# The third stage's order: the gate's priority, the row load's priority and size, and the priority of the columns' low part

## The chip, the cores and the metric

The kernel runs on one core of a Trainium2 chip. Its time is the device time of one execution in microseconds (us). Before the change three runs gave 611.12, 612.05 and 613.5 us, a median of 612.05. The engines are named as in the profile: PE (TensorE's matmuls), PEld (its weight loads), DVE (VectorE), ACT (ScalarE), POOL (GpSimd) and SP (which here only issues transfers).

## The reference, cut to what matters

```python
attn = scan(x, a, B, C)                    # 4 batches x 8 heads x 768 steps x 32
x = attn.reshape(3072, 256)                # rows of 256

h = x @ w_in                               # 256 -> 2048
g = P3(h) / (Q2(h) + 1e-6)                 # a cubic over a quadratic, by element
x = g @ w_out                              # 2048 -> 256

logits = norm(x) @ norm(expert_emb).T / tau    # 3072 x 8
idx, w = argmax(logits), softmax(logits)[argmax]
for e in range(8):                         # w1[e] 256 x 1024, w2[e] 1024 x 256
    rows = idx == e
    out[rows] = w[rows] * (relu(x[rows] @ w1[e]) @ w2[e])
```

## The kernel before

Stage 1 (the scan) and stage 2 (the dense layers, 3072 rows in blocks) fill PE up to about 425 us; stage 2 also scatters each row, with its eight logits and its number, into a table in HBM ordered by expert. **Stage 3** takes the experts one after the other from that table and is what the change touches. A *slot* is an expert by its rank in row count, a tile is 128 rows, a *pass* is one slot's turn over some tiles.

The first three passes (`first_pass`, names `f...`: `fh` the hidden product, `fr` its ReLU, `fy` the output product, `fg` the rows) take two tiles each of slots 0, 1 and 2 with plain weights. The later passes (`run_pass`) are, in order, 0_2, 1_2, 2_2 (two tiles, starting at tile 2), 4_0, 5_0, 6_0, 7_0 (three tiles), 3_0 (twice two tiles). Names carry slot, first tile and chunk: `eh0_2_3` is slot 0, from tile 2, chunk 3 of the 1024 hidden units.

In a later pass each matrix is split into a high and a low part, and a product is made of three matmuls, high by high, high by low, low by high.

- **Weights** (L930 to L953): a load by SP into one of four buffers "raw" (`ra` for w1, `rb` for w2, L946), the high part by ACT (`eah`, `ebh`, L947), and the low part by a subtract of 128x512 on DVE or on POOL, whichever the planner finds free (`eal`, `ebl`, L950). The first passes' rows `fg` use the same four buffers until their last tile is delivered.
- **Rows** (L955 to L979): one load per pass by SP into one of three buffers `g` (L961); for each tile two transposes on PE into a PSUM bank (`t3`, L969; two such banks, which `ck` at L1180 uses too), the high part of the columns by ACT (`xh`, L972), the low part by DVE (`xl`, L975).
- **Gate** (L981 to L1009): from the rows, the norm and the logits, a chain of small steps between ACT (`jk`, L990, L995, L996, L1005) and DVE (L994, L997 to L1004, L1006 to L1008) that ends in the weight `gt` per row.
- **Hidden chunks** (L1011 to L1034): six matmuls into `eh` (L1023; PSUM, four banks), ReLU `hh` on ACT (L1025), the rest `hl` on DVE (L1026), then matmuls into `y` (L1032). Each pass has eight chunks.
- **Delivery** (L1036 to L1056): `y` times `gt` into `yo`, by ACT (L1046) or DVE (L1048), and an indirect transfer of the tile to `out`, issued by POOL (L1052).

**What sets the order.** Every instruction is recorded with `op(engine, duration, at, ...)`. `Plan.run` then replays them in a model of the five engines: an engine that is free takes the ready instruction with the smallest `at` whose buffers are free. `size` tells this model how long a transfer occupies it, and `port=True` (among these lines on L950 alone) that DVE and POOL exclude each other. The engines run the order that comes out; what the model thinks of times is gone by then, and only the waits on data and buffers remain. So a changed `at` can move any instruction that is ready at about the same model time. `sh(at, late, early)` adds `late` to `at` in stage 3.

Of the kernel before, what the change touches and what calls it, by code (L numbers as in the profile page):

```python
# [17 lines left out]
P = 128  # L18
# [10 lines left out]
ROW = DM + NE + 1  # L29
# [26 lines left out]
def sh(at, late, early):  # L56

    return at + (early if at < 4 else late)
# [16 lines left out]
class Plan:  # L75
# [29 lines left out]
    def op(self, eng, us, at, fn, r=(), w=(), lag=0.0, size=0, after=(), port=None):  # L105

        port = {None: ("POOL",), True: ("POOL", "DVE"), False: ()}[port]
        o = dict(port=port, on=eng if isinstance(eng, dict) else {eng: us}, any=isinstance(eng, dict), at=at, fn=fn, lag=lag, size=size, i=len(self.ops))
        deps = set()
        vals = {}
        for x, wr in [(x, False) for x in r] + [(x, True) for x in w]:
            v, s = x if isinstance(x, tuple) else (x, None)
            vals[id(v)] = v
            hit = lambda z: z[1] is None or s is None or z[1] == s
            deps.update(z[0] for z in v.wr if hit(z))
            if wr:  # L120
                deps.update(z[0] for z in v.rd if hit(z))
        for x, wr in [(x, False) for x in r] + [(x, True) for x in w]:
            v, s = x if isinstance(x, tuple) else (x, None)
            if wr:
                if s is None:
                    v.wr, v.rd = [], []
                else:
                    v.wr = [z for z in v.wr if z[1] != s]
                    v.rd = [z for z in v.rd if z[1] != s]
                v.wr.append((o["i"], s))  # L130
            else:
                v.rd.append((o["i"], s))
        deps.update(z[0] for v in after for z in v.wr + v.rd)
        deps.discard(o["i"])
        o["deps"] = deps
        o["vals"] = list(vals.values())
        for v in o["vals"]:
            v.left += 1
        self.ops.append(o)
        return o  # L140
# [135 lines left out]
def ssm_ffn_moe_kernel(  # L276
# [18 lines left out]
    D = nc.sync.dma_start  # L295
    plan = Plan()
    op = plan.op

    def act(n, k=0):
        return 0.06 + n / 1200 + 0.09 * k  # L300
# [5 lines left out]
    def dve(n, k=0):  # L306
        return 0.069 + n / 960 + 0.06 * k
# [20 lines left out]
    def bank(name, shape=(P, 512)):  # L328
        return plan.val(ps_s, list(shape), F32, name, "s", S_B, True)
# [95 lines left out]
    xs = dram.tile([NE * CAP, ROW], F32, name="xs")  # L425
    xs_v, xs_c = Val(tile=xs), Val(tile=xs)
# [97 lines left out]
    at = 26.0  # L524
# [340 lines left out]
    ranked = Val()  # L865
# [48 lines left out]
    one, two = Val(), Val()  # L914
# [40 lines left out]
    def tokens(e, t0, n, at):  # L955

        nm = f"{e}_{t0}"
        g = plan.val(sp, [P, TPE, ROW], F32, f"g{nm}", "g", 3)
        xh, xl = (plan.val(sp, [P, 2, TPE * P], FR, f"x{z}{nm}", f"x{z}", 2) for z in "hl")
        r0 = lambda: expert[e] * CAP + t0 * P  # L960
        op("SP", 0.47, sh(at - 4, 6.12, 0), lambda: D(out=g[:, 0:n, :], in_=xs[bass.ds(r0(), n * P), :].rearrange("(t p) c -> p t c", p=P)), r=[xs_v, xs_c, two, ranked], w=[g], size=n * P * ROW * 4)  # L961
        for t in range(n):
            tr = bank(f"t3_{nm}_{t}")
            o = slice(t * P, (t + 1) * P)
            tv = lambda tr=tr: tr[:, 0:256].rearrange("p (k t) -> p k t", k=2)

            def f(t=t, tr=tr):
                for k in range(2):
                    T.transpose(out=tr[:, k * P:(k + 1) * P], in_=g[:, t, k * P:(k + 1) * P], identity=ident.t)  # L969

            def f1(o=o, tv=tv):
                A.activation(out=xh[:, :, o], in_=tv(), func=AF.Copy)  # L972

            def f2(o=o, tv=tv):
                V.tensor_tensor(out=xl[:, :, o], in0=tv(), in1=xh[:, :, o].bitcast(F32), op=ALU.subtract)  # L975
            op("PE", 0.218, at - 2 + 0.3 * t, f, r=[g, ident], w=[tr])
            op("ACT", act(256), sh(at - 2 + 0.3 * t, 0.08, 0), f1, r=[tr], w=[(xh, t)])
            op("DVE", dve(256), sh(at - 2 + 0.3 * t, 6.92, 0), f2, r=[tr, (xh, t)], w=[(xl, t)])
        return g, xh, xl  # L979

    def gate(plan, nm, g, n, at, pool):  # L981
# [76 lines left out]
    def run_pass(e, t0, parts, at):  # L1058

        nm = f"{e}_{t0}"  # L1060
        g, xh, xl = tokens(e, t0, sum(parts), at)
        gt = gate(plan, nm, g, sum(parts), at + 1, sp)
        q = 0
        for n in parts:
            nm = f"{e}_{t0 + q}"
            y = [plan.val(*z, True) for z in [(ps_a, [P, 512], F32, f"y{nm}_{b}", "acc", 2) for b in range((n + 1) // 2)]]
            for f in range(8):
                hidden(nm, e, q, n, f, xh, xl, y, at + f * n / 4)
            at += 2 * n
            deliver(nm, q, n, g, y, gt, at + 0.9)  # L1070
            q += n
# [78 lines left out]
    at = S3  # L1150
    held = None
    for j, (e, t0, parts) in enumerate(FIRST + THEN):
        if j == len(FIRST):
            for g in range(NG - LATE, NG):
                route(g, NF * (g + 1) + 2)
            at += 4
        if j < len(FIRST):
            first_pass(e, EARLY, NF * (NG - 1) + 2 + 2 * j, 92.0 if j < SMALL else at, 1.2 if j < SMALL else 0.5, j < SMALL)
            at += 2 * EARLY if j >= SMALL else 0
            continue  # L1160
        if e != held:
            for i in range(8):
                weights(e, i, at - 7 + i, f"{e}_{t0}")
            held = e
        run_pass(e, t0, parts, at)
        at += 2 * sum(parts)
# [46 lines left out]
    with tc.If(n_over > 0), tc.tile_pool(name="ovp", bufs=1) as ovp:  # L1213
        def ot(shape, dt, name):
# [42 lines left out]
            out=ro, in0=lane[:, None, :].to_broadcast([P, NCH, P]), in1=sf[:, 1, :, None].to_broadcast([P, NCH, P]), op=ALU.is_equal,  # L1257
        )
        with tc.For_i(0, n_over, 1) as i:
# [14 lines left out]
            for k in range(2):  # L1274
                G.indirect_dma_start(
                    out=wa[:, k, :], out_offset=None, in_=w1.rearrange("e d f -> (e d) f"),
                    in_offset=bass.IndirectOffsetOnAxis(ap=wi[:, k:k + 1], axis=0),
                )
            for k in range(8):
                G.indirect_dma_start(  # L1280
                    out=wb[:, k, :], out_offset=None, in_=w2.rearrange("e f d -> (e f) d"),
# [20 lines left out]
            gt = gate(rest, "o", Val(tile=go), 1, 0.0, ovp)  # L1302
            rest.run()
            tr = ps_s.tile([P, 512], F32, name="tro", tag="s")
# [12 lines left out]
            for f in range(8):  # L1317
# [4 lines left out]
                out=out, out_offset=bass.IndirectOffsetOnAxis(ap=ti[:, 1:2], axis=0), in_=yv, in_offset=None,  # L1322
# [4 lines left out]
    with tc.If(n_odd > 0):  # L1327
        y_d = dram.tile([DM, NT], F32, name="y_d")
        with tc.tile_pool(name="gp", bufs=1) as gp:
# [30 lines left out]
        with tc.tile_pool(name="gq", bufs=1) as gq:  # L1360
# [21 lines left out]
            with tc.For_i(0, NT, 512) as t0:  # L1382
# [19 lines left out]
                for t in range(4):  # L1402
                    tr = ps_s.tile([P, 512], F32, name="trg", tag="s")
# [77 lines left out]
```

## Time and profile before

| | |
|---|---|
| median of three runs | 612.05 us (611.12 to 613.5) |
| the profiled execution | 609.87 us |
| its span, first to last instruction | 608.1 us |
| busy: PE, DVE, ACT, POOL | 550.6, 485.2, 467.4, 243.9 us |
| mean granted clock of PE | 0.973 of 2.4 GHz |
| from 430 to 444 us, PE busy | 14.00 of 14.00 us |
| from 556.0 to 595.6 us, PE busy | 39.60 of 39.60 us |
| from 595.6 us to the end of the span | 12.5 us, PE busy 0.02 |

The profiled execution's time is its span and 1.77 us around it. Shares of busy time are means over the whole span; the change lies in the last 180 us, so the views below are cut to windows there. In a timeline each row has a start, a duration, the engine, the line, the operation and its tiles; what stands in square brackets is how long the engine had been idle before it and what ended that.

### The profile page before, as it was taken

Reading aid. Unit: us, or ns where it says so; the run is one execution under the profiler, and the core shown is the slowest. Engines: PE = TensorE matmul, PEld = TensorE weight load, DVE = VectorE, ACT = ScalarE, POOL = GpSimd, SP = SyncE. Lnnn points to the kernel's source line nnn. Section 1 sums busy time; section 2 is a strip of 40 time slices with the busy share of each in tenths; the row PEclk is TensorE's granted clock in tenths of the full one; section 3 lists DMA queues with packets and bytes.
Section 4 is the critical chain, followed back from the end, with each engine's and each line's share of the span. In section 5 each row is a group of like instructions: output and inputs, shape, how many; then the busy total and the mean of one; then the engine's idle time right before and its main releaser. Section 6 shows DMA issues by size and latency. Waiting matters only on the chain.

```text
span 608.1 us, 10413 instructions
## 1 busy us (share of the span) xinstructions
PE 550.6 (91%) x3429; PEld 428.0 (70%) x3429; DVE 485.2 (80%) x994; ACT 467.4 (77%) x940; POOL 243.9 (40%) x229
## 2 busy tenths in 40 slices
PE   1567989999999999999999999899979979999991
PEld 0234656776667676767676786677869879999991
DVE  7998899889889998999899889883467676777430
ACT  6899989999999999989989997973255666566330
POOL 2573334445444544463454436342413442122111
PEclk9868999999999999999999999999999989999996
DMA  7960606122103110210010011961445645554000
GB/s 247 390 204 19 180 9 179 26 70 81 45 0 97 40 58 19 75 59 1 2 66 9 0 37 36 301 204 54 138 157 163 211 146 173 174 153 141 19 23 14
DMA packets 47919, 61.08 MB, mean 100 GB/s; under 512 B 4135, under 2 KB 37776, under 8 KB 47856
## 3 DMA queue, kind: packets, MB, share of 16 engines
q1 hardware_dynamic: 45360, 53.92, 28.9%
q0 software_dynamic: 2496, 6.41, 3.0%
q8 instruction: 29, 0.48, 0.3%
q14 instruction: 34, 0.28, 0.2%
HBM read 46.11 MB, written 14.72 MB: 100 GB/s over the span
## 4 chain that ended last, share of the span: by engine, by line
PE 53%; issue 14%; DVE 8%; DMA 7%; POOL 4%; ACT 3%; SPq 1%; POOLq 0%; DVEq 0%; ACTq 0%
PE acc L764 19%; PE h L738 19%; PE c L666 3%; DMA g<-xs 3%; PE y L706 2%; POOL out_dram L1052 2%; PE eh L1023 2%; PE fy L1118 1%; PE y L712 1%; PE tk L801 1%; PE y L1032 1%; DVE gh L752 1%; DMA out_dram<-yo,g 1%; DMA fg<-xs 1%; DVE u L753 1%
## 5 line engine op out<-in xcount | busy, mean ns | idle before, releaser
L755 POOL TENSOR_TENSOR gl<-p,v 128x512 fp32r<-128x512 f32 x96 | 126.8, 1324 | 173.7 <-DVE p L754 60.6
L738 PE MATMUL h<-x1h,wiw 128*128 128x512 f32 x384 | 142.0, 413 | 9.0 <-DVE p L754 5.9
L764 PE MATMUL acc<-gh,wow 128*128 128x512 f32 x384 | 112.0, 413 | 0.0
L738 PEld LDWEIGHTS h<-x1h,wiw 128*128 128x128 f32 x384 | 73.7, 192 | 35.3 <-DVE p L754 7.5
L764 PEld LDWEIGHTS acc<-gh,wow 128*128 128x128 f32 x384 | 67.9, 188 | 29.5 <-issue 15.9
L753 DVE SCALAR_TENSOR_TENSOR u<-u,lq,gh 128x512 f32<-128x512 f32 x96 | 81.1, 845 | 0.8
L752 DVE SCALAR_TENSOR_TENSOR gh<-h,as,v 128x512 fp32r<-128x512 f32 x96 | 71.6, 746 | 12.5 <-ACT v L750 12.0
L738 PE MATMUL h<-x1l,wiw 128*128 128x512 f32 x192 | 76.9, 401 | 0.0
L747 DVE SCALAR_TENSOR_TENSOR h<-p,sl,h 128x512 f32<-128x512 f32 x96 | 71.8, 749 | 6.0 <-ACT v L744 5.7
L743 ACT ACTIVATE p<-h,kk 128x512 f32<-128x512 f32 x96 | 65.3, 680 | 14.6 <-POOL gl L755 8.7
L754 DVE SCALAR_TENSOR_TENSOR p<-h,as,u 128x512 f32<-128x512 f32 x96 | 71.5, 745 | 3.0 <-DVE bw L651 0.2
L745 ACT ACTIVATE u<-v,qb 128x512 f32<-128x512 f32 x96 | 69.5, 724 | 1.5
L749 ACT ACTIVATE v<-u,lq 128x512 f32<-128x512 f32 x96 | 69.3, 722 | 1.6
L750 ACT ACTIVATE v<-v 128x512 f32<-128x512 f32 x96 | 60.4, 629 | 1.0
L764 PE MATMUL acc<-gl,wow 128*128 128x512 f32 x192 | 60.6, 396 | 0.1
L744 ACT ACTIVATE v<-h 128x512 f32<-128x512 f32 x96 | 56.9, 593 | 2.5 <-POOL gl L755 2.5
L1026 DVE SCALAR_TENSOR_TENSOR hl<-eh,hh 128x256 fp32r<-128x256 f32 (+1 forms) x72 | 34.3, 480 | 26.7 <-ACT hh L1025 26.2
L1032 PE MATMUL y<-ebh,hh 128*128 128x256 f32 x176 | 51.2, 291 | 1.3 <-ACT hh L1025 1.3
L1052 POOL DMA_INDIRECT out_dram<-yo,g x22 | 22.9, 1040 | 71.7 <-DVE yo L1048 51.6
L1032 PE MATMUL y<-ebh,hl 128*128 128x256 f32 x176 | 50.4, 286 | 1.1 <-DVE hl L1026 1.1
L1025 ACT ACTIVATE hh<-eh 128x256 fp32r<-128x256 f32 (+1 forms) x72 | 30.4, 424 | 26.0 <-PE eh L1023 23.5
L1032 PE MATMUL y<-ebl,hh 128*128 128x256 f32 x176 | 49.8, 283 | 0.0
(238 smaller groups left out, 1137.1 us busy)
## 6 DMA issues: line engine op xcount, KB each, us to landing
ra<-in_w SPq DMA_DIRECT2D x32, 256.0 KB, 3.0
rb<-in_w SPq DMA_DIRECT2D x32, 256.0 KB, 3.0
xb<-in_xb SPq DMA_DIRECT2D x12, 384.0 KB, 4.0
xs<-empty SPq DMA_DIRECT2D x8, 530.0 KB, 6.8
wiwr<-in_w_in SPq DMA_DIRECT2D x8, 512.0 KB, 7.3
wowr<-in_w_out SPq DMA_DIRECT2D x8, 512.0 KB, 7.5
xrow<-row SPq DMA_DIRECT2D x6, 530.0 KB, 3.6
bc<-in_bct SPq DMA_DIRECT2D x12, 256.0 KB, 2.8
```

The lines of the kernel that those rows point to most:

```text
L738: T.matmul(out=h.t, lhsT=part(wiw[g_], z)[:, k, fs], rhs=xx[:, k, :], start=(k == 0 and e == 0), stop=(k == 1 and e == 2))
L743: op("ACT", act(512, 1), s, lambda: A.activation(out=pp.t, in_=h.t, func=AF.Square, bias=kk.t), r=[h, kk], w=[pp])
L745: op("ACT", acts(512) + 0.06, s + 0.3, lambda: A.activation(out=uu.t, in_=vv.t, func=AF.Square, bias=qb.t), r=[vv, qb], w=[uu])
L747: op("DVE", dve(512, 1), s + 0.8, lambda: stt(out=h.t, in0=pp.t, scalar=sl.t, in1=h.t, op0=ALU.add, op1=ALU.mult), r=[h, pp, sl], w=[h])
L749: op("ACT", acts(512) + 0.09, s + 0.9, lambda: A.activation(out=vv.t, in_=uu.t, func=AF.Ln, bias=lq.t), r=[uu, lq], w=[vv])
L750: op("ACT", acts(512), s + 1.0, lambda: A.activation(out=vv.t, in_=vv.t, func=AF.Exp, scale=-1.0), r=[vv], w=[vv])
L752: op("DVE", dve(512, 1), s + 1.5, lambda: stt(out=gh.t, in0=h.t, scalar=as_.t, in1=vv.t, op0=ALU.add, op1=ALU.mult), r=[h, as_, vv], w=[gh])
L753: op("DVE", dve(512, 1), s + 1.6, lambda: stt(out=uu.t, in0=uu.t, scalar=lq.t, in1=gh.t.bitcast(F32), op0=ALU.add, op1=ALU.mult), r=[uu, l ...
L754: op("DVE", dve(512, 1), s + 1.7, lambda: stt(out=pp.t, in0=h.t, scalar=as_.t, in1=uu.t, op0=ALU.add, op1=ALU.subtract), r=[h, as_, uu], w ...
L755: op("POOL", pool2(512), s + 2.1, lambda: G.tensor_tensor(out=gl.t, in0=pp.t, in1=vv.t, op=ALU.mult), r=[pp, vv], w=[gl])
L764: T.matmul(out=acc[dh].t, lhsT=part(wow[g_], z)[:, i % 2, dh * P:(dh + 1) * P], rhs=x.t, skip_group_check=True, start=(i == 0 and e == 0), ...
L1032: T.matmul(out=y[t // 2][:, t % 2 * DM:(t % 2 + 1) * DM], lhsT=hx[:, o], rhs=wb[w][:, f % 2, :], start=(f == 0 and i == 0 and t % 2 == 0), ...
```

## The change

Three numbers of the order are changed; no computation is.

1. The rows' load (L961): its priority goes from `at - 4` with 6.12 added to `at - 6`, and the planner's model takes twice its real size.
2. The columns' low part (L975): 6.92 is no longer added to its priority, so that it follows 0.3 per tile from `at - 2`.
3. The gate (call at L1062): from `at + 1` to `at + 2 * parts[0] - 2`, which is `at + 2` in the passes of two tiles and 3_0, `at + 4` in those of three.

```diff
--- before.py
+++ after.py
@@ -958,7 +958,7 @@
         g = plan.val(sp, [P, TPE, ROW], F32, f"g{nm}", "g", 3)
         xh, xl = (plan.val(sp, [P, 2, TPE * P], FR, f"x{z}{nm}", f"x{z}", 2) for z in "hl")
         r0 = lambda: expert[e] * CAP + t0 * P
-        op("SP", 0.47, sh(at - 4, 6.12, 0), lambda: D(out=g[:, 0:n, :], in_=xs[bass.ds(r0(), n * P), :].rearrange("(t p) c -> p t c", p=P)), r=[xs_v, xs_c, two, ranked], w=[g], size=n * P * ROW * 4)
+        op("SP", 0.47, at - 6.0, lambda: D(out=g[:, 0:n, :], in_=xs[bass.ds(r0(), n * P), :].rearrange("(t p) c -> p t c", p=P)), r=[xs_v, xs_c, two, ranked], w=[g], size=2 * n * P * ROW * 4)
         for t in range(n):
             tr = bank(f"t3_{nm}_{t}")
             o = slice(t * P, (t + 1) * P)
@@ -975,7 +975,7 @@
                 V.tensor_tensor(out=xl[:, :, o], in0=tv(), in1=xh[:, :, o].bitcast(F32), op=ALU.subtract)
             op("PE", 0.218, at - 2 + 0.3 * t, f, r=[g, ident], w=[tr])
             op("ACT", act(256), sh(at - 2 + 0.3 * t, 0.08, 0), f1, r=[tr], w=[(xh, t)])
-            op("DVE", dve(256), sh(at - 2 + 0.3 * t, 6.92, 0), f2, r=[tr, (xh, t)], w=[(xl, t)])
+            op("DVE", dve(256), at + -2.0 + 0.3 * t, f2, r=[tr, (xh, t)], w=[(xl, t)])
         return g, xh, xl
 
     def gate(plan, nm, g, n, at, pool):
@@ -1059,7 +1059,8 @@
 
         nm = f"{e}_{t0}"
         g, xh, xl = tokens(e, t0, sum(parts), at)
-        gt = gate(plan, nm, g, sum(parts), at + 1, sp)
+
+        gt = gate(plan, nm, g, sum(parts), at + 2 * parts[0] - 2.0, sp)
         q = 0
         for n in parts:
             nm = f"{e}_{t0 + q}"
```

In the changed file a blank line shifts all lines behind L1061 by one (L1114 is L1115 there). The order on SP is the same but for one small load of a register that trades places with its neighbour. On PE two output products of pass 0_2 stand one chunk later. What moves is on DVE, ACT and POOL. Of the 64 subtracts of L950, 16 were on POOL and 20 are now.

On ScalarE, around the last first pass, the first delivery of slot 1 (`yo1_0_0`) stands ahead of two `jk` and two small steps of a gate that it stood behind, the ReLUs `fr2_0_3` and `fr2_0_6` have gone to VectorE, and the two `xh0_2` stand back to back behind `eah1_2_1`, where `ebh0_2_3` stood between them. Further on, `hh2_2_0` stands ahead of the first `jk4_0`, and stood behind it.

VectorE, around the last first pass (slot 2) and the start of pass 0_2; before:

```order
L1114 TENSOR_SCALAR fr2_0_5_5033<-fh2_0_5_5009 128x256
L950 TENSOR_TENSOR ebl1_2_0_5035<-rb1_2_0_4986,ebh1_2_0_5031 128x512
L950 TENSOR_TENSOR eal0_2_3_5043<-ra0_2_3_4993,eah0_2_3_5037 128x512
L950 TENSOR_TENSOR eal1_2_1_5056<-ra1_2_1_5023,eah1_2_1_5052 128x512
L1114 TENSOR_SCALAR fr2_0_7_5061<-fh2_0_7_5045 128x256
L975 TENSOR_TENSOR xl0_2_5069<-t3_0_2_0_5058,xh0_2_5067 128x2x128
L950 TENSOR_TENSOR ebl0_2_3_5078<-rb0_2_3_5041,ebh0_2_3_5071 128x512
L975 TENSOR_TENSOR xl0_2_5069<-t3_0_2_1_5073,xh0_2_5067 128x2x128
```

and after:

```order
L1115 TENSOR_SCALAR fr2_0_5_5029<-fh2_0_5_4996 128x256
L1007 TENSOR_SCALAR gt1_2_5023<-gt1_2_5023 128x2
L1008 RECIPROCAL gt1_2_5023<-gt1_2_5023 128x2
L1115 TENSOR_SCALAR fr2_0_6_5040<-fh2_0_6_5025 128x256
L1115 TENSOR_SCALAR fr2_0_7_5057<-fh2_0_7_5037 128x256
L975 TENSOR_TENSOR xl0_2_5063<-t3_0_2_0_5054,xh0_2_5061 128x2x128
L975 TENSOR_TENSOR xl0_2_5063<-t3_0_2_1_5069,xh0_2_5061 128x2x128
```

Four subtracts (`ebl1_2_0`, `eal0_2_3`, `eal1_2_1`, `ebl0_2_3`) no longer stand between the first pass's ReLUs and the columns `xl0_2`; one more ReLU (`fr2_0_6`) and two steps of a gate do.

GpSimd in the same place, where the deliveries of slots 0, 1 and 2 are issued (`fg` the rows whose buffer a delivery frees); before:

```order
L1052 DMA out_0_dram<-yo0_0_1_4851,fg0_0_4311 3072x256
L1052 DMA out_0_dram<-yo1_0_0_4952,fg1_0_4373 3072x256
L1052 DMA out_0_dram<-yo1_0_1_4968,fg1_0_4373 3072x256
L950 TENSOR_TENSOR ebl1_2_1_5104<-rb1_2_1_5050,ebh1_2_1_5081 128x512
L1052 DMA out_0_dram<-yo2_0_0_5106,fg2_0_4431 3072x256
L1052 DMA out_0_dram<-yo2_0_1_5116,fg2_0_4431 3072x256
```

and after:

```order
L1052 DMA out_0_dram<-yo0_0_1_4851,fg0_0_4311 3072x256
L1052 DMA out_0_dram<-yo1_0_0_4941,fg1_0_4373 3072x256
L1052 DMA out_0_dram<-yo1_0_1_4949,fg1_0_4373 3072x256
L950 TENSOR_TENSOR ebl0_2_2_4992<-rb0_2_2_4917,ebh0_2_2_4985 128x512
L950 TENSOR_TENSOR ebl1_2_0_5042<-rb1_2_0_5000,ebh1_2_0_5035 128x512
L950 TENSOR_TENSOR eal0_2_3_5050<-ra0_2_3_5009,eah0_2_3_5044 128x512
L950 TENSOR_TENSOR eal1_2_1_5065<-ra1_2_1_5018,eah1_2_1_5048 128x512
L1052 DMA out_0_dram<-yo2_0_0_5100,fg2_0_4431 3072x256
L1052 DMA out_0_dram<-yo2_0_1_5115,fg2_0_4431 3072x256
```

Three of the subtracts that left VectorE stand here now, with `ebl0_2_2`, as a block of four between two deliveries; `ebl1_2_1` left POOL.

VectorE at the start of pass 4_0, where that pass's gate meets the last chunks of pass 2_2; before:

```order
L1026 SCALAR_TENSOR_TENSOR hl2_2_3_5624<-eh2_2_3_5590,hh2_2_3_5611 128x256
L1000 TENSOR_SCALAR sq4_0_5553<-sq4_0_5553 128x3
L1001 RECIPROCAL rc4_0_5569<-sq4_0_5553 128x3
L1004 TENSOR_TENSOR ex4_0_5529<-ex4_0_5529,rc4_0_5569 128x24
L1026 SCALAR_TENSOR_TENSOR hl2_2_4_5648<-eh2_2_4_5617,hh2_2_4_5638 128x256
L975 TENSOR_TENSOR xl4_0_5654<-t3_4_0_0_5634,xh4_0_5646 128x2x128
```

and after:

```order
L1026 SCALAR_TENSOR_TENSOR hl2_2_3_5620<-eh2_2_3_5582,hh2_2_3_5609 128x256
L997 RECIPROCAL rc4_0_5626<-sq4_0_5596 128x3
L998 TENSOR_TENSOR rc4_0_5626<-rc4_0_5626,s24_0_5534 128x3
L999 TENSOR_TENSOR sq4_0_5596<-sq4_0_5596,rc4_0_5626 128x3
L1000 TENSOR_SCALAR sq4_0_5596<-sq4_0_5596 128x3
L1001 RECIPROCAL rc4_0_5626<-sq4_0_5596 128x3
L1026 SCALAR_TENSOR_TENSOR hl2_2_4_5647<-eh2_2_4_5613,hh2_2_4_5635 128x256
L975 TENSOR_TENSOR xl4_0_5652<-t3_4_0_0_5631,xh4_0_5644 128x2x128
```

Before, the gate's steps L997 to L999 stood further ahead, each between chunks of 2_2 and two subtracts, and `ex4_0` (L1004) ahead of `hl2_2_4`; now L997 to L1001 are one block behind `hl2_2_3`, and `ex4_0` comes behind the first `xl4_0`.

## Rows read from the trace of the kernel before

**Rows 1.** Waits of TensorE, 430 to 608: line waited for, total us, times, longest.

```profile
PE t L969 <- DVE xl L975: 3.5, 1, 3.5
PE ck L1180 <- DVE xl L975: 2.0, 1, 2.0
PE y L1032 <- ACT hh L1025: 1.3, 1, 1.3
PE y L1032 <- DVE hl L1026: 1.1, 2, 0.6
```

**Rows 2.** Windows: stretch, us, busy (instructions) of each engine, granted clock, DMA share, GB/s.

```profile
452.00:455.40 3.40, 1.35 (x10) 0.99 (x9) 1.90 (x5) 2.04 (x5) 0.00 (x0) 1.00 0.63 187
455.40:458.90 3.50, 3.50 (x17) 3.29 (x16) 3.36 (x13) 0.67 (x2) 2.08 (x2) 0.51 0.46 139
483.00:489.60 6.60, 5.29 (x43) 4.93 (x43) 4.60 (x15) 5.51 (x18) 2.24 (x2) 1.00 0.37 113
489.60:493.00 3.40, 0.34 (x3) 0.14 (x2) 3.33 (x5) 0.26 (x2) 2.63 (x3) 1.00 0.47 140
493.00:496.40 3.40, 2.97 (x14) 2.97 (x15) 2.38 (x9) 2.05 (x5) 0.25 (x1) 0.50 0.82 255
```

**Rows 3.** Timeline of TensorE: last first pass and start of pass 0_2.

```profile
454.84 0.24 PE L1180 MATMUL ck<-oh,ones 128*128 128x8 bf16 x4 [2.05 <-DVE xl L975]
...
455.96 0.78 PE L1023 MATMUL eh<-xh,eah 128*128 128x256 f32 x1
...
456.75 0.41 PE L1023 MATMUL eh<-xh,eal 128*128 128x256 f32 x1
456.96 0.41 PE L1023 MATMUL eh<-xh,eah 128*128 128x256 f32 x1
...
459.11 0.28 PE L1023 MATMUL eh<-xh,eal 128*128 128x256 f32 x1
459.23 0.28 PE L1023 MATMUL eh<-xh,eah 128*128 128x256 f32 x1
```

**Rows 4.** Timeline of ScalarE there.

```profile
444.70 0.45 ACT L1046 ACTIVATE yo<-fy,gt 128x256 f32<-128x256 f32 x1
...
452.77 0.63 ACT L947 ACTIVATE eah<-ra 128x512 fp32r<-128x512 f32 x1 [1.16 <-DMA ra<-in_w]
...
454.80 0.37 ACT L972 ACTIVATE xh<-t 128x256 fp32r<-128x256 f32 x1
```

**Rows 5.** Timeline of GpSimd there.

```profile
446.71 0.97 POOL L1052 DMA_INDIRECT out_dram<-yo,fg  x1 [0.31 <-DVE eal L950]
```

**Rows 6.** Timeline of SP there: loads' issue.

```profile
447.46 3.08 SPq L946 DMA_DIRECT2D ra<-in_w  x2
```

**Rows 7.** Chain that ended last, there: start, us, what.

```profile
450.17 2.58 DMA ra<-in_w
```

**Rows 8.** Timeline of VectorE there.

```profile
453.43 0.69 DVE L950 TENSOR_TENSOR eal<-ra,eah 128x512 fp32r<-128x512 f32 x1 [1.37 <-ACT eah L947]
...
454.93 0.69 DVE L950 TENSOR_TENSOR ebl<-rb,ebh 128x512 fp32r<-128x512 f32 x1
455.54 0.42 DVE L975 TENSOR_TENSOR xl<-t,xh 128x256 fp32r<-128x256 f32 x1
```

**Rows 9.** Line L950 on GpSimd, 435 to 608: count: min/median/max ns.

```profile
L950 POOL TENSOR_TENSOR eal<-ra,eah x7: 1276/1288/1310, 466.5 to 552.7; 128x512 fp32r<-128x512 f32 x7
```

**Rows 10.** Timeline of VectorE at the start of pass 4_0.

```profile
489.15 3.13 DVE L1000 TENSOR_SCALAR sq<-sq 128x3 f32<-128x3 f32 x1
...
492.96 0.42 DVE L975 TENSOR_TENSOR xl<-t,xh 128x256 fp32r<-128x256 f32 x1
```

**Rows 11.** Timeline of GpSimd at the start of pass 4_0.

```profile
489.76 1.28 POOL L950 TENSOR_TENSOR eal<-ra,eah 128x512 fp32r<-128x512 f32 x1
490.98 1.27 POOL L950 TENSOR_TENSOR ebl<-rb,ebh 128x512 fp32r<-128x512 f32 x1
```

**Rows 12.** Groups by form, 430 to 608: count, busy us, mean ns, idle before.

```profile
L998 DVE TENSOR_TENSOR rc<-rc,s 128x4 f32<-128x4 f32 x1 | 1.2, 1199 | 0.0
```

## The prediction

> **What bounds the kernel now.** The change lies in stage 3, so I read the waits of TensorE from 430 us on, then the windows around the longest, then the timelines of the engines in them. TensorE is busy without a gap through most of this stage; its waits are few, and four lines hold nearly all of them: 3.5 us before a transpose of pass 4_0, 2.0 before `ck`, 1.3 before an output product, and twice together 1.1 before another [rows 1]. All but the 1.3 end with VectorE. What the change is worth must come out of these 7.9 us and out of what follows them: behind the 2.0 the granted clock is 0.51 for 3.5 us, behind the 3.5 it is 0.50 for 3.4 us, and around the 1.3 it stays 1.00 [rows 2]; 0.5 is the lower of the two levels, 1.2 GHz of 2.4. At that level matmuls of a chunk start 0.21 us apart (456.75, 456.96), at the higher 0.12 (459.11, 459.23) [rows 3].
>
> **The rows' load (1).** The order on SP is the same but for one register load, so the earlier priority moves no transfer: the loads go out when their buffer comes free. The doubled size lives only in the planner's model. I cost the edit itself at nothing; what it does, it does by the other engines' order.
>
> **Columns and deliveries around 445 to 460 (2 and 3).** This is the largest term. Before, the chain runs: ScalarE makes `yo1_0_0` at 444.70 [rows 4], the second of slot 1's deliveries is issued by GpSimd at 446.71 [rows 5], and its end frees the buffer for the second of two loads on SP [rows 6], `ra1_2_1`, whose transfer takes from 450.17 to 452.75 [rows 7], 3.46 us behind the delivery's issue. ScalarE then has `eah1_2_1` at 452.77, and `xh0_2`, which is queued behind it, has its second half only at 454.80 [rows 4]. On VectorE the second `xl0_2` follows at 455.54, behind `ebl0_2_3` of 0.69 us, and ends at 455.96 [rows 8], where the first chunk of pass 0_2 starts [rows 3].
>
> After, `yo1_0_0` stands ahead of two `jk` and two small steps of a gate that it stood behind: I put it 1.5 us earlier, at 443.2, and the delivery's issue 1.7 earlier, at 445.0, because the subtract that stood in front of it is ordered away too. With the same 3.46 us the buffer would be free at 448.5. SP issues in order, and the load ahead of it (447.46 [rows 6]) waits for a buffer that `ebl0_2_2` frees, now a subtract on GpSimd of 1.29 us where VectorE took 0.69 [rows 8, 9]; that puts it at 448.2 and `ra1_2_1` at 448.8. It lands 2.58 later, at 451.4 (451.9 if the four subtracts on GpSimd hold anything up): 0.9 to 1.4 before now. Behind it `eah1_2_1` (0.63), two `xh0_2` (0.37 each), two `xl0_2` (0.42 each) with no subtract between: the last ends at 453.2 to 453.7. `ck` and the four matmuls of `fy` stand before the first chunk, which took from 454.84 to 455.96, 1.1 us [rows 3]; the first bank is free one `xl0_2` sooner, so the chunk starts at about 454.45. **Term: -1.5** (between -1.0 and -1.9).
>
> TensorE's one idle stretch of 2.05 us is then two of about 1.1 and 0.8. The trace has one idle stretch of 1.3 without a fall of the clock [rows 1, 2] and two of 2.05 and 3.49 us with one, so I take the clock to hold. The 17 matmuls of the window 455.4 to 458.9 [rows 2] then start 0.12 instead of 0.21 us apart [rows 3]: 17 x 0.094 = 1.6. **Term: -1.6** (0 if the clock falls all the same).
>
> Given back: pass 0_2's first output product needs `hl0_2_0`, and VectorE now has `ebl0_2_3` and `ebl1_2_1` ahead of it, which it had before or not at all; one of them, 0.69 [rows 8], is not covered by anything on TensorE. **Term: +0.7** (0 to 1.4).
>
> **The gate of pass 4_0 (3).** Before, one small step of the gate, `sq4_0` of 128x3 (L1000), holds VectorE from 489.15 for 3.13 us, to 492.28 [rows 10]. Beside it GpSimd runs two subtracts end to end, 489.76 to 492.25 [rows 11]; the step ends when they have. Behind it wait two more steps, `hl2_2_4` and the first `xl4_0`, which starts 0.68 later at 492.96 [rows 10]; the transposes need its bank and start after 3.49 us [rows 1]. After, the block L997 to L1001 stands at about the same time behind `hl2_2_3`, and the first of its steps with two operands in memory meets `eal4_0_3` on GpSimd, which is still followed by `ebl4_0_2`. I let GpSimd start them 0.7 sooner, about half of the 1.3 us that go ahead of it (below): VectorE is free at 491.6, the three steps left and `hl2_2_4` take 0.9 where two steps and `hl2_2_4` took 0.68, and `xl4_0` of 0.42 ends at 492.9; the transposes start some 0.4 sooner than now. **Term: -0.4.** The bounds are wide: if the block passes before GpSimd's first subtract, VectorE runs on and the whole wait goes with the slow clock behind it, -3.5 and, for the 14 matmuls in the slow stretch [rows 2], 14 x 0.094 = -1.3, in all -4.8; if all four steps are held, each behind a subtract of its own, two more subtracts come on top, +2.6. I take the middle that is nearest the row, because the same engines meet in the same order.
>
> The Trainium skill (SBUF — State Buffer, Who interferes with whom) has a rule for this: of VectorE and GpSimd the one that issues first has the shared ports for its whole instruction, and the other is blocked until then. By that rule the step would have waited for one instruction. The trace agrees on the block but not on its length: the step stayed blocked past a second start on GpSimd at 490.98 [rows 10, 11]. With one subtract alone VectorE would come free 1.3 us sooner, this term would be -1.7, and the sum 607.5 us in place of 608.8.
>
> The 1.3 us before an output product [rows 1] is `hh2_2_0` queued on ScalarE behind a gate's `jk4_0` that waits for its rows; in the new order it stands ahead. That wait goes, but TensorE then only comes sooner to the same blocked `xl4_0`, which is late next. **Term: 0.**
>
> **Later passes.** The smaller of the two waits for `hl` [rows 1] is about 0.4 (1.1 less 0.6 and rounding), at the turn from 4_0 to 5_0; the low part there now stands ahead of two subtracts. **Term: -0.4.** The larger, 0.6, comes from the gate step that took 1.2 us behind a single subtract on GpSimd [rows 12]. That subtract (`eal3_0_1`) is VectorE's now, but one at the turn before it (`eal7_0_1`) is GpSimd's: the same price a pass earlier. **Term: 0.** The four subtracts on GpSimd between pass 4_0 and 5_0 cost 5.2 us there [rows 9], beside work of TensorE that is full; nothing, unless a step of VectorE needs its ports (rival 2).
>
> **Sum.** -1.5 - 1.6 + 0.7 - 0.4 - 0.4 = -3.2 us against the profiled execution's 609.87: 606.7. The median of the runs shown is 2.2 above that execution, so on its scale 612.05 - 3.2 = **608.8 us**.
>
> **Rivals.**
> 1. *The clock falls at pass 0_2 all the same, or the loads bind.* For it: two idle stretches stand close together there, and the load before `ra1_2_1` comes later by GpSimd's slower subtract. Against it: the 1.3 us at 484. Then the 1.6 is not won: 610.4 us, no measurable change.
> 2. *VectorE is starved behind GpSimd's rows of subtracts: slower.* The order has two rows of four where before there were at most two side by side. For it: two end to end already held one small step for 3.13 us [rows 10, 11]. Four take 5.2 us; a gate step or a low part that arrives at their start while TensorE's next product hangs on it adds at least what two did: 3.5 of waiting and 1.3 of slow clock, 4.8. From one such stall on it decides, since the gains are 3.2: 612.05 - 3.2 + 4.8 = 613.7 us, with two 618.5. Against it: around 448 VectorE's work is mostly ReLUs out of PSUM, whose wait TensorE has 0.6 us or less of so far.
> 3. *Pass 4_0's stall dissolves.* For it: the gate's steps move to another place, and only a few tenths decide who comes first. Against it: they stay within the same 4 us. Then 4.8 less 0.4 more is won: 604.4 us.
> 4. *It doesn't do what it says.* The load that is to go sooner doesn't; if only noise in the order is left, the time is 612 within 1 us.
>
> **How the numbers follow.** The forecast has 0.40, rival 1 0.22, rival 2 0.16, rival 3 0.14, rival 4 0.08. Half a per cent, 3.06 us, is about what a measurement can tell from no change here. The forecast lies 3.25 below the median and so at that edge: 0.25 of its 0.40 count as faster, with 0.14 of rival 3 and 0.05 of rival 1 that is 0.44. Slower is rival 2 less the part that the gains make up for, 0.15 of 0.16 with the width of the measurement against it and a little from rival 4: 0.17. The rest, 0.39, is no change. The forecast's own range is 607 to 610.4, from the bounds of its terms. For 8 in 10 it is drawn down to rival 3 and up to one stall of rival 2: 603.9 to 613.8.
>
> **What would show it.** In the profile after: `ck` at 453 to 453.5 and the first chunk of 0_2 at 454 to 455; granted clock 1.00 from 455 to 459; the wait before the transposes of 4_0 still 3 us or more, behind a gate step of over 2 us on VectorE; no wait of TensorE over 1.5 us elsewhere; the wait of 1.3 at 484 gone. I am wrong if a wait of several us stands anywhere that has none now, or if the clock between 455 and 459 is still 0.5.

## The result and the profile after

The changed kernel took 606.98 us (median of 15 runs, 601.0 to 610.85) beside 611.12 (15 runs, 608.21 to 617.55) for the kernel before: ratio 0.9901, 95% interval 0.9877 to 0.9926 (the two medians alone give 0.993). In two later sessions the same pair gave 0.9911 (0.9885 to 0.9936) and 0.9941 (0.9911 to 0.9970). So the change takes off 0.6 to 1.0%, some 3.6 to 6 us (2.8 to 5.4 by the medians alone). Forecast were 3.2: the right sign, but less than the intervals of the first two sessions allow (4.5 to 7.5 and 3.9 to 7.0 us).

The profiled execution of the changed kernel lasts 609.72 us (span 607.9), no less than before's 609.87. That is no contradiction. The order is the same on every engine up to about 440 us, so up to there the executions differ by chance alone. One chunk of the first passes on TensorE, in the kernel before and then in the changed one (timeline: start, duration):

```profile
420.94 1.11 PE L1108 MATMUL fh<-fx,fa 128*128 128x256 f32 x4
```

```profile
426.15 1.57 PE L1109 MATMUL fh<-fx,fa 128*128 128x256 f32 x4
```

The changed kernel's profile came there 5.2 us late and ended 0.2 early: 5.4 us were won behind this point (5.9 from the second matmul of this chunk to the last one of the kernel). Over the first twelve profiles of the table below, the second matmul of this chunk starts anywhere between 419.5 and 426.7 us. A comparison of two profiled executions must therefore start at a common row near the change.

TensorE's waits in the changed kernel, 420 us to the end, answer to [rows 1]:

```profile
PE t L969 <- DVE xl L975: 3.6, 1, 3.6
PE ck L1181 <- DVE xl L975: 1.4, 1, 1.4
PE tk L799 <- ACT row L804: 1.2, 1, 1.2
PE y L1032 <- ACT hh L1025: 0.3, 1, 0.3
PE y L1032 <- DVE hl L1026: 0.2, 1, 0.2
```

The 3.5 us before the transposes of 4_0 are still there; the 1.3 for `hh` is gone (the 0.3 stands elsewhere), the 1.1 for `hl` has shrunk to 0.2; `ck` waits 1.4 in place of 2.0. (`tk` belongs to the part before the change.) The windows around `ck` and around 4_0, as in [rows 2]:

```profile
455.40:458.90 3.50, 2.14 (x15) 1.68 (x15) 1.50 (x6) 2.12 (x5) 2.79 (x3) 1.00 0.43 115
458.90:462.40 3.50, 3.50 (x32) 3.50 (x31) 2.90 (x9) 2.59 (x7) 2.17 (x2) 1.00 0.74 206
490.00:494.40 4.40, 0.85 (x8) 0.65 (x6) 4.26 (x10) 1.32 (x4) 3.06 (x3) 1.00 0.46 129
494.40:497.80 3.40, 3.39 (x20) 3.39 (x21) 1.99 (x8) 2.21 (x6) 2.50 (x2) 0.64 0.89 272
```

Behind `ck` the granted clock now stays at 1.00, and 32 matmuls run in 3.5 us where 17 ran; behind 4_0 it falls as before. Around `ck`, the changed kernel's timeline of ScalarE:

```profile
456.30 0.63 ACT L947 ACTIVATE eah<-ra 128x512 fp32r<-128x512 f32 x1 [0.46 <-DMA ra<-in_w]
456.84 0.64 ACT L972 ACTIVATE xh<-t 128x256 fp32r<-128x256 f32 x2
```

of VectorE:

```profile
457.24 0.76 DVE L975 TENSOR_TENSOR xl<-t,xh 128x256 fp32r<-128x256 f32 x2 [2.22 <-ACT xh L972]
```

and of GpSimd:

```profile
448.99 0.97 POOL L1052 DMA_INDIRECT out_dram<-yo,fg  x1 [0.30 <-DVE gt L1006]
```

From `eah1_2_1` to the end of the second `xl0_2` it is 1.7 us (456.30 to 458.00), where it was 3.2 (452.77 to 455.96 [rows 4, 8]): the two columns now follow each other. For the rest, count from the second matmul of the chunk above, at 421.24 and 426.72. The delivery is issued 22.3 us behind it (448.99), where it was 25.5 (446.71 [rows 5]), and `eah1_2_1` starts 29.6 us behind it (456.30), where it was 31.5 (452.77 [rows 4]). So delivery and weight both come sooner, the weight by less, since from the one to the other it is now 7.3 us and was 6.1.

At 4_0 the picture is that of [rows 10, 11] with another gate step in it, `L998` of 128x3. VectorE:

```profile
490.18 2.93 DVE L998 TENSOR_TENSOR rc<-rc,s 128x3 f32<-128x3 f32 x1
```

and GpSimd beside it:

```profile
490.59 1.28 POOL L950 TENSOR_TENSOR eal<-ra,eah 128x512 fp32r<-128x512 f32 x1
491.80 1.27 POOL L950 TENSOR_TENSOR ebl<-rb,ebh 128x512 fp32r<-128x512 f32 x1
```

### The profile page after: what moved, and what is told of

Same layout as the page of the kernel before. It is cut to its first block, busy times and chain, and to the rows that moved or that the text cites. A ratio compares the mean times of both kernels' runs of the same rounds, so it can differ in the third digit from the quotient of the medians.

```text
span 607.9 us, 10415 instructions
## 1 busy us (share of the span) xinstructions
PE 555.0 (91%) x3429; PEld 430.0 (71%) x3429; DVE 478.7 (79%) x989; ACT 467.1 (77%) x941; POOL 249.7 (41%) x233
## 4 chain that ended last, share of the span: by engine, by line
PE 59%; issue 8%; DMA 7%; DVE 7%; ACT 4%; POOL 3%; SPq 1%; another core or an unknown queue 0%; POOLq 0%; ACTq 0%
PE h L738 19%; PE acc L764 19%; PE eh L1023 4%; PE y L1032 4%; PE c L666 3%; DMA g<-xs 2%; PE y L706 2%; PE y L712 2%; DMA ra<-in_w 2%; POOL out_dram L1052 1%; PE tk L801 1%; PE fy L1119 1%; DMA out_dram<-yo,g 1%; DMA fa<-in_w 1%; DVE gh L752 1%
## 5 line engine op out<-in xcount | busy, mean ns | idle before, releaser
L764 PEld LDWEIGHTS acc<-gh,wow 128*128 128x128 f32 x384 | 68.0, 188 | 29.6 <-issue 15.9
L753 DVE SCALAR_TENSOR_TENSOR u<-u,lq,gh 128x512 f32<-128x512 f32 x96 | 78.9, 822 | 0.8
```

What stands on the lines that cost most here:

```text
L753: op("DVE", dve(512, 1), s + 1.6, lambda: stt(out=uu.t, in0=uu.t, scalar=lq.t, in1=gh.t.bitcast(F32), op0=ALU.add, op1=ALU.mult), r=[uu, l ...
L764: T.matmul(out=acc[dh].t, lhsT=part(wow[g_], z)[:, i % 2, dh * P:(dh + 1) * P], rhs=x.t, skip_group_check=True, start=(i == 0 and e == 0), ...
```

## Which of the edits moves the order

This needs no run: each edit alone, set beside the kernel before, row by row on every engine. The load's earlier priority alone gives the order of before. The columns' new priority alone gives the order of before. The doubled size alone gives the changed kernel's order but for eight rows on ACT, DVE and POOL, all where pass 4_0 begins; doubled size and columns' priority together give the changed kernel's order exactly, so the gate's new priority adds nothing to them. (Alone, the gate's priority moves rows from pass 4_0 on, and others than the change does.) What is timed first below is therefore a number in the planner's model of a transfer, nothing that the chip is told.

## The experiments

**The doubled size alone.**

```diff
-        op("SP", 0.47, sh(at - 4, 6.12, 0), ..., w=[g], size=n * P * ROW * 4)
+        op("SP", 0.47, sh(at - 4, 6.12, 0), ..., w=[g], size=2 * n * P * ROW * 4)
```

> Of the change only the doubled size of the rows' load in the planner's model; priorities of load, columns and gate as before. On ACT, DVE and POOL its order differs from the changed kernel's in eight rows, all at pass 4_0. Theory A (the doubled size alone makes the gain): ratio to before 0.990 +- 0.003, and in the trace the wait before ck 1.4 us, granted clock 1.00 behind it, the 3.5 us before the transposes of 4_0 still there. Rival B (the gate's or the columns' new priority is needed): at most a third of the gain, 0.997 or above.

Ratio 0.9963 (0.9936 to 0.9990): a gain, but less than theory A's, and less than the changed kernel's in its own session. So it was run again beside the changed kernel.

> The kernel of size_only once more, now beside the changed kernel in one session. It came out at 0.996, the changed kernel at 0.990 and 0.991, though their orders differ in eight rows at pass 4_0. Theory A (those rows, which the columns' new priority moves, are worth 2 to 3 us): 0.994 to 0.997 and 0.003 or more above the changed kernel beside it. Rival B (the rows are worth nothing, the executions scatter): within 0.002 of it.

> The changed kernel, unaltered, as the partner of the other three. Ratio 0.989 to 0.993; in the profile the waits that all its profiles had (3.5 us before the transposes of 4_0, about 1 before ck, none for hl above 0.3 in the later passes), and clock 1.00 at the start of 0_2.

0.9947 (0.9919 to 0.9975) beside 0.9941 (0.9911 to 0.9970), the changed kernel a little above what was expected of it; medians 604.70 and 605.51. Rival B of the repeat holds: the eight rows are worth nothing that was measured here, though intervals of 0.003 either way would hide 1.8 us. But for these rows the doubled size alone is the change. Its waits in the repeat, at the same two places:

```profile
PE t L969 <- DVE xl L975: 3.7, 1, 3.7
PE ck L1180 <- DVE xl L975: 0.9, 1, 0.9
```

**Early passes alone, later passes alone.** The size is doubled only for 0_2, 1_2 and 2_2 (first kernel), only for the passes from 4_0 on (second).

```diff
-        ..., size=n * P * ROW * 4)
+        ..., size=(2 if t0 == 2 else 1) * n * P * ROW * 4)    # size_first
+        ..., size=(1 if t0 == 2 else 2) * n * P * ROW * 4)    # size_later
```

> The doubled size only for the loads of passes 0_2, 1_2 and 2_2; all else as before. Theory A (two thirds or more of the gain comes from the order around 444 to 497 us, where the first pass's ReLUs and the columns xl0_2 no longer stand behind subtracts): ratio 0.992 to 0.994, no wait of TensorE for fr, wait before ck 1.4, clock 1.00 at the start of 0_2; the 0.4 and 0.6 us waits for hl at the later turns stay. Rival B (the gain is spread over the later passes): 0.997 or above.

> The doubled size only for the loads of passes 4_0, 5_0, 6_0, 7_0 and 3_0; all else as before, so the order around 444 to 460 is before's. Theory A: ratio 0.996 to 0.998 (the waits of 0.4 and 0.6 us for hl go, some 1.3 to 1.6 us), the 2.05 us before ck and the clock of 0.5 behind it stay. Rival B: 0.993 or below.

0.9976 (0.9953 to 0.9999) and 0.9977 (0.9959 to 0.9996), in the session in which both together (size_only) gave 0.9963. Each half is worth some 1.4 us, with intervals from about nothing to 2.9. Theory A's two thirds for the first half is not borne out, and its profile has a wait of 1.0 us for `fr` that was to be gone. The second half's ratio came as theory A expected, but not its reason in full: a wait of 0.6 for `hl` is left, and `ck` waited 1.54 with the clock at 1.00, not 2.05 with 0.5 behind it.

**The changed kernel again, and its block of four subtracts put back on VectorE.**

```diff
-            {"DVE": dve(512), "POOL": pool2(512)}, 0, sh(at, 7.77, 0),
+            {"DVE": dve(512)} if f"e{k}l{nm}_{q}" in ("ebl0_2_2", "ebl1_2_0", "eal0_2_3", "eal1_2_1") else {"DVE": dve(512), "POOL": pool2(512)}, 0, sh(at, 7.77, 0),
```

> The changed kernel once more, unaltered, beside the next three and for a second profile of it. Ratio to before between 0.989 and 0.996. If the gain is a matter of order alone (theory A), its stage 3 from the first pass's chunk at 421 us to the end is again some 4 to 6 us shorter than before's; if part of the 5.6 us there was only made up for a late start (rival B), it is 3 to 4.5 us with a wait before ck or fr that the first profile lacked.

> The changed kernel with the four subtracts that stand as a block on GpSimd between the deliveries of slots 1 and 2 (ebl0_2_2, ebl1_2_0, eal0_2_3, eal1_2_1) bound to VectorE; the later order of passes 4_0 to 3_0 is as in the changed kernel. Theory A (that block on GpSimd is what lets xl0_2 and the ReLUs come in time): the wait before ck returns to about 2 us and the clock behind it to 0.5, 2 to 3.5 us above the changed kernel. Rival B (the block on GpSimd costs as much as it gives, since gate steps on VectorE are held behind it): within 1 us of the changed kernel.

0.9911 (0.9885 to 0.9936) and 0.9925 (0.9898 to 0.9952). From the chunk to the last matmul the changed kernel's second profile is 5.1 us shorter than before's, as its theory A said, with the wait for `fr` that its rival B named. The two kernels' medians, 603.87 and 604.80, are 0.9 us apart: rival B by the time, though the intervals are too wide to exclude theory A's 2 us. The trace says that theory A's mechanism is there, and what is paid for it. With the four on VectorE, TensorE's waits:

```profile
PE t L969 <- DVE xl L975: 3.5, 1, 3.5
PE ck L1180 <- DVE xl L975: 2.2, 1, 2.2
...
PE fy L1118 <- DVE fr L1114: 0.2, 1, 0.2
```

and the window behind `ck`:

```profile
457.00:460.50 3.50, 3.50 (x22) 3.32 (x22) 2.08 (x10) 2.13 (x6) 1.59 (x2) 0.73 0.54 152
```

The 2 us before `ck` and a slow clock behind it are back. With the four on GpSimd, the second profile of the changed kernel has on TensorE:

```profile
450.08 1.13 PE L1118 MATMUL fy<-fb,fr 128*128 128x256 f32 x4 [0.98 <-DVE fr L1114]
```

on VectorE:

```profile
447.60 0.83 DVE L998 TENSOR_TENSOR rc<-rc,s 128x2 f32<-128x2 f32 x1
...
449.61 0.41 DVE L1114 TENSOR_SCALAR fr<-fh 128x256 f32<-128x256 f32 x1
```

and on GpSimd:

```profile
447.16 1.26 POOL L950 TENSOR_TENSOR ebl<-rb,ebh 128x512 fp32r<-128x512 f32 x1 [2.58 <-ACT sq L996]
```

A gate step is held behind `ebl0_2_2` until 448.43; the other steps of that gate and of a second one come next on VectorE, and the ReLU `fr` only at 449.61: TensorE waits 1.0 us. That is the prediction's second rival, at a fifth of its price. The first profile of the changed kernel, with the late TensorE, had no such wait.

**The gate's priority alone.**

```diff
-        gt = gate(plan, nm, g, sum(parts), at + 1, sp)
+        gt = gate(plan, nm, g, sum(parts), at + 2 * parts[0] - 2.0, sp)
```

> Of the change only the gate's priority. By its order nothing moves before pass 4_0; there eal4_0_3 goes from GpSimd to VectorE and L998 and L999 come behind it, eal5_0_0, ebl5_0_0, ebl6_0_0 and eal6_0_1 go to GpSimd. Theory A: only one subtract is left beside pass 4_0's gate, so the wait before its transposes falls from 3.5 to 1.5 to 2.5 us: ratio 0.995 to 0.999. Rival B (the freed subtract only shifts the block): 0.999 to 1.002 with the wait at 3 us or more.

0.9949 (0.9926 to 0.9971), theory A by the wait and at its edge by the ratio. TensorE's waits:

```profile
PE t L969 <- DVE xl L975: 1.9, 1, 1.9
PE ck L1180 <- DVE xl L975: 1.7, 1, 1.7
```

the window behind `ck`:

```profile
453.40:456.90 3.50, 3.50 (x27) 3.04 (x24) 3.40 (x9) 2.15 (x6) 1.32 (x2) 1.00 0.50 156
```

and at pass 4_0 VectorE:

```profile
485.60 0.15 DVE L998 TENSOR_TENSOR rc<-rc,s 128x3 f32<-128x3 f32 x1
...
486.27 1.25 DVE L999 TENSOR_TENSOR sq<-sq,rc 128x3 f32<-128x3 f32 x1
```

with GpSimd beside it:

```profile
486.21 1.29 POOL L950 TENSOR_TENSOR ebl<-rb,ebh 128x512 fp32r<-128x512 f32 x1
```

With `eal4_0_3` on VectorE one subtract is left on GpSimd, a gate step is held 1.25 us in place of 3.13, and the transposes wait 1.9. The window also shows what one profile can hide: the order here is before's until 4_0, yet `ck` waited 1.7 and the clock stayed at 1.00, there and behind the 1.9 at 4_0.

**The two subtracts beside 4_0's gate on VectorE**, in the kernel before and twice in the changed one.

```diff
-            {"DVE": dve(512), "POOL": pool2(512)}, 0, sh(at, 7.77, 0),
+            {"DVE": dve(512)} if f"e{k}l{nm}_{q}" in ("eal4_0_3", "ebl4_0_2") else {"DVE": dve(512), "POOL": pool2(512)}, 0, sh(at, 7.77, 0),
```

> The kernel before with eal4_0_3 and ebl4_0_2 bound to VectorE, nothing else of the change. Theory A (the wait before the transposes of 4_0 is VectorE held behind these two subtracts, whatever else the order is): the wait goes from 3.5 to under 1 us and the clock behind it stays 1.00, 3.5 to 5 us off before: ratio 0.992 to 0.995. Rival B (the gain of 7 us seen with the two on VectorE in the changed kernel is needed together with the change): 0.997 or above.

> The changed kernel, with the two subtracts eal4_0_3 and ebl4_0_2, which stand end to end on GpSimd beside the gate of pass 4_0, bound to VectorE. Theory A (the 3.6 us before the transposes of 4_0 are VectorE blocked behind these two): the long gate step shrinks to 0.2 us, the wait of 3.6 to at most 1.2, the clock behind it stays 1.00: 3 to 4.5 us off the changed kernel, ratio to before 0.983 to 0.986. Rival B (the columns are late for another reason, such as the rows' load of 4_0, and the blocked step is only in its shadow): the wait stays 2.5 us or more, ratio 0.988 to 0.992. Rival C (the freed time is lost again behind the two subtracts of 0.7 us each, now ahead of the low parts on VectorE): wait 1.5 to 2.5, ratio 0.986 to 0.989.

> The kernel of sub4_vector once more beside the changed kernel. Theory A (the 3.5 us and the slow clock behind them are paid in every execution of the changed kernel and in none of this one): no wait before the transposes of 4_0, clock 1.00 behind it, 0.005 to 0.009 below the changed kernel. Rival B (what is won there is lost again in most executions, in another wait as in sub4_before, where 1.9 us stood before a product of 2_2): a wait of 1.5 us or more behind 490, and within 0.003 of the changed kernel.

In the kernel before: 0.9924 (0.9904 to 0.9944), theory A; its median of 604.18 us stands beside 603.87 of the changed kernel in that session, so the two subtracts alone gave as much as the whole change. In the changed one: 0.9904 (0.9875 to 0.9933), then 0.9858 (0.9808 to 0.9908) with a median of 599.70 us beside 605.51 of the changed kernel in that session, 1.0% less: the fastest kernel here. The first ratio is rival B's, though its profile has no wait at 4_0 at all; the changed kernel was not run in that session. So the size of the gain rests on the second alone.

The edit moves more than the two subtracts: in both kernels the transposes that stalled now stand behind an output product of six matmuls (0.7 us) that they stood ahead of, and one load on SP goes out one place sooner. Some 0.7 us of the shorter wait may be due to that new place on TensorE. The second profile in the changed kernel has, of TensorE's waits:

```profile
PE t L969 <- DVE xl L975: 0.2, 1, 0.2
```

on VectorE the step that was held 2.93 us, and a later one:

```profile
485.99 0.16 DVE L998 TENSOR_TENSOR rc<-rc,s 128x3 f32<-128x3 f32 x1
...
488.14 1.17 DVE L1004 TENSOR_TENSOR ex<-ex,rc 128x24 f32<-128x24 f32 x1
```

on GpSimd:

```profile
487.98 1.29 POOL L950 TENSOR_TENSOR eal<-ra,eah 128x512 fp32r<-128x512 f32 x1 [2.06 <-PE t L969]
```

and in the windows behind:

```profile
487.00:490.40 3.40, 3.20 (x28) 3.00 (x27) 3.33 (x12) 2.47 (x7) 2.32 (x2) 1.00 0.56 152
490.40:493.80 3.40, 3.40 (x25) 3.40 (x25) 1.77 (x8) 1.96 (x6) 0.25 (x1) 1.00 0.93 308
```

The stall and the slow clock are gone together, and the two low parts stand ahead of `L1004`, which is held later but with nothing of TensorE behind it. In the kernel before the same edit also takes the stall (3.5 to 0.6), but gives 1.9 back in a new wait, behind a step held by the next subtract on GpSimd. TensorE's wait:

```profile
PE y L1032 <- ACT yo L1046: 1.9, 1, 1.9
```

VectorE:

```profile
496.61 1.26 DVE L1000 TENSOR_SCALAR sq<-sq 128x3 f32<-128x3 f32 x1
```

GpSimd:

```profile
496.57 1.28 POOL L950 TENSOR_TENSOR eal<-ra,eah 128x512 fp32r<-128x512 f32 x1 [1.10 <-ACT eah L947]
```

**The planner told of the gate.**

```diff
-        dv = lambda us, fn, r, w: plan.op("DVE", us, sh(at, 0.85, 0), fn, r=r, w=w)
+        dv = lambda us, fn, r, w: plan.op("DVE", us, sh(at, 0.85, 0), fn, r=r, w=w, port=True)
```

> The changed kernel with one more number for the planner: the gate's steps on VectorE are recorded as excluding GpSimd (port=True), as the subtracts are. By its order both xl4_0 of the first two tiles come ahead of L998, and eal4_0_3 goes to VectorE. Theory A (what holds the columns is the gate's steps behind GpSimd's subtracts, and the planner only has to know it): wait before the transposes of 4_0 under 1 us, clock 1.00 behind it, ratio 0.982 to 0.987. Rival B (the gate then waits in the order for GpSimd, and the deliveries and the rows' buffers come later): 0.988 or above, with a new wait of 1 us or more for hh, hl or yo.

0.9969 (0.9936 to 1.0001), beside 0.9941 (0.9911 to 0.9970) for the changed kernel: rival B's ratio, but none of its waits for `hh`, `hl` or `yo` is there. The intervals overlap, and the medians are the other way round, 604.81 and 605.51, so neither a gain nor a loss against the changed kernel is shown. The stall at 4_0 did go, to 0.9, but the order changed from 385 us on, in the gates of the first passes and around `ck` as well. Waits:

```profile
PE ck L1180 <- DVE xl L975: 2.4, 1, 2.4
PE t L969 <- DVE xl L975: 0.9, 1, 0.9
```

and the window behind `ck`:

```profile
456.50:460.00 3.50, 3.50 (x16) 3.27 (x15) 2.94 (x10) 2.01 (x4) 1.78 (x3) 0.53 0.60 165
```

**All profiles side by side.** Waits of TensorE in us at five places, read from its timeline, and the times from the second matmul of the chunk above to the first matmul of pass 0_2 and to the start of the last matmul (in before 421.24 to 455.96 and to 595.35). "Order" is that of passes 0_2 to 2_2, before's (b), the changed kernel's (c), or an order of its own (-); in gate_port six small matmuls (0.6 us) that otherwise stand ahead of the chunk stand behind it.

| profile | order | `fr` | `ck` | `hh` near 484 | 4_0 | `hl`, from 505 | chunk to 0_2 | chunk to last |
|---|---|---|---|---|---|---|---|---|
| before | b | 1.2 | 2.05 | 1.3 | 3.5 | 1.15 | 34.7 | 174.1 |
| size_later | b | 1.4 | 1.54 | 0 | 3.0 | 0.6 | 33.9 | 170.0 |
| gate_only | b | 0.3 | 1.66 | 0.2 | 1.9 | 1.8 | 32.9 | 168.6 |
| sub4_before | b | 1.1 | 1.41 | 0 | 0.6 | 0.5 | 33.5 | 168.8 |
| after | c | 0 | 1.36 | 0 | 3.6 | 0.2 | 31.9 | 168.2 |
| after_again | c | 1.25 | 0.95 | 0 | 3.5 | 0.2 | 33.0 | 169.0 |
| after_3 | c | 1.35 | 0.91 | 1.6 | 3.6 | 0.2 | 33.1 | 172.4 |
| size_only | c | 2.0 | 0.64 | 0 | 3.7 | 0.3 | 33.5 | 169.9 |
| size_only_2 | c | 0 | 0.86 | 0 | 3.7 | 0.2 | 31.2 | 168.7 |
| size_first | c | 1.0 | 0.73 | 0 | 3.2 | 1.4 | 32.5 | 170.8 |
| sub4_vector | c | 0.1 | 1.25 | 0 | 0 | 0.2 | 31.9 | 162.8 |
| sub4_vector_2 | c | 1.3 | 1.42 | 0 | 0.2 | 0.2 | 33.6 | 165.1 |
| four_vector | - | 0.2 | 2.20 | 0 | 3.5 | 0.2 | 33.8 | 169.4 |
| gate_port | - | 0.2 | 2.37 | 0 | 0.9 | 0.1 | 34.1 | 166.9 |

## Why the prediction was right or wrong

- **The rows' load: wrong about what the edit is.** "I cost the edit itself at nothing" held for the transfers, whose order on SP is the same. But the doubled size alone moves the order, and beside it the gate's and the columns' priorities, to which the terms were written, move it not at all or by eight rows without a measured effect. Only an order built with one edit at a time shows that.
- **First chunk of 0_2, -1.5: about right in size, one step failed.** The term was the start of that chunk. Behind the common matmul it comes at 33.7 us in before's order and at 32.6 in the changed one (means of the table; the ranges overlap): 1.2 sooner. (In the first pair of profiles it is 2.9.) The delivery's issue comes 1.9 us sooner in the mean, where 1.7 was put; but from it to `eah1_2_1` it is 7.8 us in the mean of the changed order, and 6.4 in before's, so the weight comes 0.4 sooner, not 0.9 to 1.4. That step failed. In five of the eight profiles the load starts within 0.03 us of the end of `ebl0_2_2` on GpSimd; the sum let that subtract hold only the load ahead, and took 2.58 us for the transfer. In the second profile of the changed kernel (chain that ended last: start, us):

```profile
447.18 1.25 POOL ebl L950
448.44 3.30 DMA ra<-in_w
```

  The next step, two columns with no subtract between, held and made up for it: from `eah1_2_1` to their end it is 1.7 us in all eight profiles, and 3.2 to 3.7 in the four of before's order. (The prediction's own durations for this stretch add up to 2.2, not to the 1.8 that it used; they overlap.) The wait before `ck` itself is 1.7 in the mean of before's order and 1.0 in the changed one, and before's profile, on which the sum was made, has the longest of its order.
- **The clock, -1.6: right, and partly luck of the profile.** It is 1.00 behind `ck` in every profile of the changed order. It fell behind waits of 2.05, 2.20 and 2.37 us, and in sub4_before behind 1.41 and then 0.36; it held behind 1.54 in size_later and 1.66 in gate_only, whose order there is before's. So it is likely that not every execution of the kernel before pays this; the kernel itself has one profile.
- **+0.7 given back: too much.** Waits for `hl` or `hh` in passes 0_2 and 1_2 are 0.2 to 0.5 us. What was not priced is `fr`: up to 1.0 us at a time behind the gate's row. The table has it in both orders, 1.0 and 0.9 in the mean, so it cancels.
- **Pass 4_0, -0.4: wrong, nothing came.** The stall is 3.5 to 3.6 us in all three profiles. The sooner start was borrowed from the 1.3 for `hh`; but that one is no property of the order: it is 0.2 and 0 in gate_only and sub4_before, whose order there is before's, and 1.6 in after_3, where `hh2_2_1` stood behind two `jk4_0` that waited for the rows. The bound of -4.8 for a stall that dissolves was of the right size: with the two subtracts on VectorE the changed kernel is 5.8 us faster in the one session that has both, and the kernel before 5.1 in its own.
- **Later passes, -0.4 and 0: the first right, the second wrong.** All `hl` waits from 505 us on fall from 1.15 to 0.2, in all three profiles of the changed kernel. "The same price a pass earlier" failed: a gate step is held 1.21 us behind `eal7_0_1` as foreseen, but TensorE has work there and waits 0.24, not 0.64. VectorE and then GpSimd in the changed kernel:

```profile
535.06 1.21 DVE L999 TENSOR_TENSOR sq<-sq,rc 128x3 f32<-128x3 f32 x1
```

```profile
534.97 1.27 POOL L950 TENSOR_TENSOR eal<-ra,eah 128x512 fp32r<-128x512 f32 x1 [10.52 <-ACT eah L947]
```

- **The rivals.** Rival 2 occurred in small (1.0 us for `fr`, not 4.8). Rival 3, the stall dissolved, was not in the change but in the experiments. Rival 1 did not occur. Rival 4's premise held, the load does not go sooner, but not its time.
- **The sum: too small.** By order, 1.2 at the first chunk, 0.9 at the later turns and up to 1.6 of clock make 2.1 to 3.7 us, where 3.6 to 6 were measured. The rest can't be placed from one profile of the kernel before; it stays open. That the time came out within 2 us of the forecast is partly luck: the +0.7 was not paid and the -0.4 at 4_0 not won, and these two nearly cancel.

## What to carry to other kernels

Where a planner makes the order, build each edit alone and compare orders before pricing any: the number that looks like a mere hint may be the whole change. Price waits from more than one execution, anchored at a row near the change; here one profile's 1.3 us for `hh` and its slow clock were partly chance. The largest wait was left untouched by the change: two subtracts bound to the other engine by name were worth as much as the change when put into the kernel before, and 5.8 us on top of it in one session. A general rule for the same exclusion moved other things too, and no gain from it is shown.

## What the runs showed of the hardware

A small step of the gate on VectorE that comes while GpSimd runs a subtract is held to that subtract's end: 1.25 us in gate_only and 1.21 in the changed kernel, where a step beside none takes 0.16. Not every step is: a reciprocal runs beside a subtract in 0.17. In gate_only, later on, two subtracts stand end to end on GpSimd:

```profile
510.08 1.28 POOL L950 TENSOR_TENSOR ebl<-rb,ebh 128x512 fp32r<-128x512 f32 x1 [10.18 <-ACT ebh L947]
511.32 1.27 POOL L950 TENSOR_TENSOR eal<-ra,eah 128x512 fp32r<-128x512 f32 x1
```

and beside them VectorE has:

```profile
510.23 1.16 DVE L1000 TENSOR_SCALAR sq<-sq 128x3 f32<-128x3 f32 x1
511.42 0.17 DVE L1001 RECIPROCAL rc<-sq 128x3 f32<-128x3 f32 x1
511.63 1.00 DVE L1004 TENSOR_TENSOR ex<-ex,rc 128x24 f32<-128x24 f32 x1
```

The first step is let through when the first subtract ends, and the third is held by the second subtract alone. At 4_0 it is otherwise: one step is held to the end of both subtracts, 3.13 us in before and 2.93 in the changed kernel. Its record there starts 0.6 and 0.4 us ahead of the first subtract, while GpSimd is still issuing a delivery, in the changed kernel this one:

```profile
489.12 1.45 POOL L1052 DMA_INDIRECT out_dram<-yo,g  x1 [0.30 <-DVE hl L1026]
```

Whether that is what makes the difference is not shown. The Trainium skill (SBUF — State Buffer, Who interferes with whom) has the second to issue blocked until the first is through; the trace agrees for the single subtracts and for the two at 510, and differs at 4_0, where the step stayed blocked through both.

The same program, in the part that is the same in the first twelve rows of the table, reached the same matmul between 419.5 and 426.7 us. Differences of a few us between two single profiles say nothing.
